# Two heads at a time: a change to the preparation of cluster-masked attention

## The chip, the cores and the metric

The kernel runs on one core of a Trainium2 chip. The metric is the device time in microseconds (us) of one execution, the median of the runs.

## The reference

Three blocks follow each other: attention in which a query sees only the keys of its own cluster, a feed-forward block with a squared ReLU, and a mixture of eight experts with a gate that is normalised over rows and columns eight times. Only the attention matters here:

```python
B, H, S, D = 2, 8, 768, 64          # 16 centroids for each head
q_n = q / (norm(q) + 1e-06); k_n = k / (norm(k) + 1e-06); c_n = centroids / (norm(centroids) + 1e-06)
q_assign = argmax(einsum('bhsd,hcd->bhsc', q_n, c_n), axis=-1)
k_assign = argmax(einsum('bhsd,hcd->bhsc', k_n, c_n), axis=-1)
mask = q_assign[:, :, :, None] == k_assign[:, :, None, :]
scores = where(mask, scale * matmul(q, k.transpose(0, 1, 3, 2)), -1e9)
attn = exp(scores - max(scores)); attn = attn / (sum(attn) + 1e-09)
out = matmul(attn, v)
```

## The kernel before

The attention stage works through 96 query tiles, six of 128 queries for each of 16 heads (`tile_steps`, L547). For each tile TensorE computes the scores of 128 queries against 768 keys (`score`, L448: four matmuls of 384 columns), VectorE takes the row maximum (L454), ScalarE the exponential (L461), TensorE transposes the result (L476, six transposes), ScalarE and VectorE take it out of PSUM as a high and a low part (L483, L489), and TensorE multiplies by the values (L501). Scores are issued three tiles ahead. High and low parts (`fp32r` tiles) stand in for one fp32 operand.

The mask is folded into the score matmul: the stacked operands `qb` and `kb` of a head hold 64 rows of data and 16 rows of marks, one for each centroid, which the preparation of the head computes. `prepare(n)` (L247) does so for a group of four heads, that is two pairs of heads; there are four groups. Its steps:

- `load`: four tiles of 128 rows (q and k of two heads each, transposed); `scale` multiplies the q tiles by 0.125; `high` (ScalarE, L268) and `low` (L273) split each.
- `sims` (L282): 24 matmuls multiply the split tiles by the split centroids. The centroid operand `z` is padded with zeros to 128 columns, so that all four tiles accumulate into the same output tile, one quarter of its partitions each.
- `turn` (L290) transposes that in 32 x 32 blocks on VectorE, `normal` (L297) multiplies by the inverse norms, `top` (L301) takes the maximum over 16 centroids, `match` (L305) compares, `back` (L309) transposes back, `earliest` (L316, L317) keeps the first of equal maxima by a matmul with a constant band, and `marks` copies 16 rows for each head into `qb` and `kb`.
- `norms` (L202) loads q and k in natural layout (`nat`), squares them, sums over 64 elements, and takes square root (L237), + 1e-6 and reciprocal.
- `stack` copies the high and low parts of a head into its stacked operands: six SBUF-to-SBUF DMAs.
- `vload` and `vsplit` bring in and split the values.

The first group is prepared before the first tile, the others beside the tiles. `plan` says for each step the tile behind which it is written; `SHIFT` and `MOVES` displace single steps by hand. For the first 72 tiles a planner orders each engine's instructions by its own estimate of when they can start, and the written order is the priority; from tile 72 on the written order holds. DMAs are issued on the SP queue, for two heads of the first group on GpSimd's queue.

Of the kernel before, what the change touches and what calls it, by code (L numbers as in the profile page):

```python
# [17 lines left out]
P = 128  # L18
# [23 lines left out]


MOVES = {
    (1, "low", 2): 2, (1, "match"): 1, (1, "sims", 1, 1): -1, (1, "turn", 1): -2, (2, "earliest", 0): -1,
    (2, "inverse"): 1, (2, "load", 1): -1, (2, "sims", 1, 1): -1, (3, "earliest", 0): -1,
    (3, "earliest", 1): -1, (3, "normal", 0): 1, (3, "sims", 0, 0): 1, (3, "sims", 1, 0): 1,
}
SHIFT = (
    {},  # L50
    dict(high=-1, low=-1, top=-1, match=-1, back=-1, vload=2, stack=-2),
    dict(
        high=-3, low=-3, sims=-3, turn=-3, top=-1, match=-1, back=-1, vload=1, vsplit=-1, stack=-1, square=-1, total=-1
    ),
    dict(high=-1, low=-1, sims=-2, turn=-2, normal=-1, vsplit=2, marks=1, square=-3, root=1),
)
# [6 lines left out]
class Kernel:  # L63
# [103 lines left out]
    def centroids(self, craw):  # L167
# [3 lines left out]
        z = self.tile("z", [P, 2, 4, 2, P], F32R, pool=self.prep)  # L171
        nc.vector.memset(f32(z), 0.0)
# [4 lines left out]
        nc.scalar.activation(ss, ss, AF.Sqrt)  # L177
        nc.vector.tensor_scalar_add(ss, ss, 1e-6)
# [10 lines left out]
        chi = self.tile("chi", [P, P], pool=self.prep)  # L189
        clo = self.tile("clo", [P, P], pool=self.prep)  # L190
        nc.vector.tensor_copy(chi.bitcast(F32R), ct[:, :P])
        nc.vector.tensor_tensor(clo, ct[:, :P], chi, op=ALU.subtract)
        for t in range(2):
            for qd in range(4):
                cols = slice(32 * (2 * t + qd // 2), 32 * (2 * t + qd // 2) + 32)
                nc.vector.tensor_copy(z[:, t, qd, 0, 32 * qd : 32 * qd + 32], chi[:, cols])
                nc.scalar.copy(z[:, t, qd, 1, 32 * qd : 32 * qd + 32], clo[:, cols])
        self.cst = z
# [3 lines left out]
    def norms(self, n, soon=False):  # L202

        nc = self.nc
        rn = self.rn[n] = self.tile("rn", [P, 24, 2], bufs=2, pool=self.prep)
        nats = {}

        def load(u):
            if n == 1:
                nats[u] = self.tile("atl" if u else "ath", [P, 12, 2, D], bufs=2)  # L210
            else:
                nats[u] = self.tile("nat", [P, 12, 2, D], bufs=2, pool=self.prep)
            b, t = divmod(n, 2)
            nc.sync.dma_start(nats[u], self.qkn[b, t, :, 12 * u : 12 * u + 12])

        def square(u):
            nat = nats[u]
# [5 lines left out]
        def total(u):  # L223
            nat = nats.pop(u)
            width = D
            while width > (1, 1, D, D // 2)[n] and n:
                width //= 2
                add = nat[:, :, :, :width]
                nc.gpsimd.tensor_tensor(add, add, nat[:, :, :, width : 2 * width], op=ALU.add)
            out = rn[:, 12 * u : 12 * u + 12]  # L230
            if width == 1:
                nc.gpsimd.tensor_copy(out.unsqueeze(3), nat[:, :, :, :1])
            else:
                nc.vector.reduce_sum(out, nat[:, :, :, :width], axis=AX.X)

        def root():
            nc.scalar.activation(rn, rn, AF.Sqrt)  # L237

        def inverse():
            add = nc.vector.tensor_scalar_add(rn, rn, 1e-6)  # L240
            if n == 1:
                self.tc.keep_in_program_order(add)
            nc.vector.reciprocal(rn, rn)

        return load, square, total, root, inverse

    def prepare(self, n, soon=False):  # L247
# [3 lines left out]
        b, t = divmod(n, 2)  # L251
        st = {}
        qa, qb, ka, kb, vv = self.heads_q, self.heads_qm, self.heads_k, self.heads_km, self.heads_v
        raw, hi, lo, vr = {}, {}, {}, {}
        alt = nc.vector if soon or n == 3 else nc.gpsimd
        busy = nc.vector if n < 2 else nc.gpsimd

        def load(qd):
            tag, bufs = ("eq", 1) if soon and qd == 3 else ("raw", 3)
            raw[qd] = self.tile(tag, [P, S], bufs=bufs, pool=self.prep)  # L260
            nc.sync.dma_start(raw[qd], self.qk[b, t, qd])

        def scale(qd):
            busy.tensor_scalar_mul(raw[qd], raw[qd], 0.125)

        def high(qd):
            hi[qd] = self.tile(f"hi{qd}", [P, S], F32R, pool=self.prep)
            nc.scalar.copy(hi[qd], raw[qd])  # L268

        def low(qd):  # L270
            lo[qd] = self.tile(f"lo{qd}", [P, S], F32R, pool=self.prep)
            eng = nc.gpsimd if qd % 2 else alt
            eng.tensor_tensor(lo[qd], raw.pop(qd), f32(hi[qd]), op=ALU.subtract)  # L273

        def sims(u, part):
            if part == 0:
                st[u] = self.ps("t", [P, 512])
            cols = slice(u * HALF, u * HALF + HALF)
            for qd in (2 * part, 2 * part + 1):
                zh, zl = self.cst[:, t, qd, 0], self.cst[:, t, qd, 1]  # L280
                for i, (z, x) in enumerate(((zh, hi[qd]), (zh, lo[qd]), (zl, hi[qd]))):
                    nc.tensor.matmul(  # L282
                        st[u][:, :HALF], z, x[:, cols], start=(qd == 0 and i == 0), stop=(qd == 3 and i == 2)
                    )

        def turn(u):
            if u == 0:
                st["sim"] = self.tile("sim", [P, 24, 2, C], pool=self.prep)
            flat = st["sim"].rearrange("p a j c -> p (a j c)")
            nc.vector.transpose(flat[:, u * HALF : u * HALF + HALF], st.pop(u)[:, :HALF])  # L290

        def wide(ap):
            return ap.unsqueeze(3).to_broadcast([P, 24, 2, C])

        def normal(u):
            cols = slice(12 * u, 12 * u + 12)
            alt.tensor_tensor(st["sim"][:, cols], st["sim"][:, cols], wide(self.rn[n])[:, cols], op=ALU.mult)  # L297

        def top():
            st["mx"] = self.tile("mx", [P, 24, 2], pool=self.prep)  # L300
            nc.vector.tensor_reduce(st["mx"], st["sim"], axis=AX.X, op=ALU.max)  # L301

        def match():
            st["eq"] = self.tile("eqb", [P, 24, 2, C], BF16, pool=self.prep)
            nc.vector.tensor_tensor(st["eq"], st["sim"], wide(st["mx"]), op=ALU.is_equal)  # L305

        def back():
            st["eqt"] = self.tile("eqt", [P, S], BF16, pool=self.prep)
            nc.vector.transpose(st["eqt"], st["eq"].rearrange("p a j c -> p (a j c)"))  # L309

        def earliest(u):
            if u == 0:
                st["rows"] = self.tile("eq", [P, S], pool=self.prep)
            ps = self.ps("t", [P, 512])
            cols = slice(u * HALF, u * HALF + HALF)
            nc.tensor.matmul(ps[:, :HALF], self.band, st["eqt"][:, cols], start=True, stop=True)  # L316
            nc.vector.tensor_scalar(st["rows"][:, cols], ps[:, :HALF], self.floor, self.floor, op0=ALU.add, op1=ALU.max)  # L317

        def stack(k):
            hd, (i, j) = 4 * n + k, divmod(k, 2)  # L320
            part = slice(64 * j, 64 * j + 64)
            q_hi, q_lo, k_hi, k_lo = hi[2 * i][part], lo[2 * i][part], hi[2 * i + 1][part], lo[2 * i + 1][part]
# [4 lines left out]
            for dst, src in (  # L327
# [3 lines left out]
                (nc.gpsimd if n == 0 and k > 1 else nc.sync).dma_start(f32(dst), f32(src))  # L331

        def marks(k):
            hd, (i, j) = 4 * n + k, divmod(k, 2)
            r0 = 64 * i + 16 * j
            rows = st["rows"]
            if hd == 0:
                nc.vector.tensor_copy(qb[hd][64:], rows[:16])
                nc.vector.tensor_copy(kb[hd][64:], rows[32:48])
                return  # L340
            nc.sync.dma_start(f32(qb[hd][64:]), rows[r0 : r0 + 16])
            nc.sync.dma_start(f32(kb[hd][64:]), rows[r0 + 32 : r0 + 48])

        def vload(i):
            vr[i] = self.tile("vraw", [P, QT, 2, D], bufs=2)
            nc.sync.dma_start(vr[i], self.v[b, 2 * t + i])

        def vsplit(k):
            i, j = divmod(k, 2)
            vt = vv[4 * n + k] = self.tile("vv", [P, QT, 2, D], F32R, bufs=4)  # L350
            busy.tensor_copy(vt[:, :, 0, :], vr[i][:, :, j, :])
# [782 lines left out]
```

## Time and profile before

| what | value |
|---|---|
| runs | 1570.94 us median of 3 (1569.94 to 1571.08) |
| profiled execution | 1570.48 us, of which the profile's span is 1568.7 us |
| TensorE busy | 1526.6 us (97% of the span) |
| VectorE, ScalarE, GpSimd busy | 898.7, 760.3 and 964.6 us (57%, 48% and 61%) |
| granted clock of TensorE | 0.995 of full speed over the span |

PE is TensorE, PEld its weight loads, DVE VectorE, ACT ScalarE, POOL GpSimd, SP the engine whose queue issues most DMAs. Busy time of matmuls is pipelined and their ends are modelled; the distance from start to start shows their pace.

### The profile page before, as it was taken

The numbers are of one execution on the slowest core, as the hardware profiler recorded it, in microseconds if no ns is written. First come the engines' busy times: TensorE is split into PE (matmuls) and PEld (weight loads), VectorE is DVE, ScalarE is ACT, GpSimd is POOL, SyncE is SP. The second block draws the span as 40 slices with busy tenths as digits, with TensorE's granted clock in tenths as the row PEclk, the third lists the DMA queues.
The fourth block names the chain that finished last, engine by engine and source line by source line (L and its number), as shares of the span: only waits on it lengthen the run. The fifth ranks groups of instructions, "written<-read, shape, count | busy, mean of one in ns | idle before, by whom it ended". The sixth has DMA issues, their size and how long they took to land.

```text
span 1568.7 us, 21863 instructions
## 1 busy us (share of the span) xinstructions
PE 1526.6 (97%) x8136; PEld 1399.6 (89%) x8136; DVE 898.7 (57%) x1573; ACT 760.3 (48%) x1416; POOL 964.6 (61%) x726
## 2 busy tenths in 40 slices
PE   4999998999999999999999999999999999999998
PEld 4888987999999988899999999999999999999997
DVE  7989889876653445644444535565445444444444
ACT  4889898866665643343333333333333333333331
POOL 5764446656664866656566666677565757575652
PEclk8999999999999999999999999999999999999999
DMA  9864440122220011112121211213121212121211
GB/s 276 196 188 102 97 125 29 54 81 81 81 108 0 1 55 68 67 54 81 56 80 58 77 66 69 78 57 121 55 81 55 81 55 81 54 81 55 81 55 41
DMA packets 26793, 124.69 MB, mean 79 GB/s; under 512 B 4448, under 2 KB 4576, under 8 KB 16448
## 3 DMA queue, kind: packets, MB, share of 16 engines
q1 hardware_dynamic: 26112, 120.95, 23.9%
q0 software_dynamic: 576, 2.36, 0.7%
q8 instruction: 64, 1.05, 0.3%
q14 instruction: 41, 0.34, 0.1%
HBM read 99.80 MB, written 3.15 MB: 66 GB/s over the span
## 4 chain that ended last, share of the span: by engine, by line
PE 87%; ACT 4%; DVE 3%; POOL 2%; issue 2%; DMA 1%; SPq 0%; ACTq 0%; POOLq 0%; DVEq 0%
PE t L135 34%; PE s L985 22%; PE y L985 11%; PE s L705 7%; PE s L448 3%; PE pv L501 3%; PE u L135 2%; PE t L476 2%; ACT e L461 1%; PE u L476 1%; DVE atl L489 1%; DVE m L454 1%; ACT ath L483 1%; POOL fa L623 0%; DMA ka<-hi 0%
## 5 line engine op out<-in xcount | busy, mean ns | idle before, releaser
L964 ACT ACTIVATE hh<-c 128x384 fp32r<-128x384 f32 x256 | 134.6, 526 | 606.1 <-PE y L985 266.4
L892 POOL TENSOR_TENSOR wl<-raw,wh 128x1024 fp32r<-128x1024 f32 x64 | 155.3, 2427 | 348.2 <-ACT wh L891 348.2
L965 DVE SCALAR_TENSOR_TENSOR hl<-c,hh 128x384 fp32r<-128x384 f32 x256 | 174.8, 684 | 172.5 <-ACT hh L964 172.5
L985 PE MATMUL s<-wh,hh 128*128 128x512 f32 x512 | 201.2, 393 | 0.0
L985 PE MATMUL s<-wl,hh 128*128 128x512 f32 x512 | 200.6, 392 | 0.0
L985 PE MATMUL s<-wh,hl 128*128 128x512 f32 x512 | 200.3, 391 | 0.0
L135 PE MATMUL t<-th,ah 128*128 128x384 f32 x512 | 171.8, 336 | 0.8 <-DVE c L1059 0.8
L135 PE MATMUL t<-tl,ah 128*128 128x384 f32 x512 | 172.0, 336 | 0.0
L135 PE MATMUL t<-th,al 128*128 128x384 f32 x512 | 171.8, 336 | 0.0
L884 POOL TENSOR_TENSOR al<-sm,ah 128x1024 fp32r<-128x1024 f32 x64 | 156.6, 2447 | 3.5 <-ACT ah L881 3.4
L882 POOL TENSOR_TENSOR al<-raw,ah 128x768 fp32r<-128x768 f32 x64 | 137.8, 2153 | 0.0
L135 PE MATMUL t<-xh,ah 128*128 128x384 f32 x384 | 129.4, 337 | 0.1
L135 PE MATMUL t<-xh,al 128*128 128x384 f32 x384 | 129.2, 336 | 0.0
L135 PE MATMUL t<-xl,ah 128*128 128x384 f32 x384 | 129.0, 336 | 0.0
L1035 DVE TENSOR_TENSOR c<-t,c 128x384 f32<-128x384 f32 x64 | 35.7, 558 | 144.9 <-PE t L135 144.9
L985 PEld LDWEIGHTS s<-wh,hl 128*128 128x128 f32 x512 | 96.1, 188 | 21.1
L985 PEld LDWEIGHTS s<-wh,hh 128*128 128x128 f32 x512 | 96.2, 188 | 11.7
L985 PEld LDWEIGHTS s<-wl,hh 128*128 128x128 f32 x512 | 96.2, 188 | 11.3
L691 POOL TENSOR_TENSOR hl<-r,hh 128x384 fp32r<-128x384 f32 x64 | 74.3, 1162 | 49.3 <-ACT r L690 46.1
L985 PE MATMUL y<-wh,hl 128*128 128x512 f32 x256 | 99.7, 390 | 0.0
L985 PE MATMUL y<-wh,hh 128*128 128x512 f32 x256 | 99.7, 389 | 0.0
L985 PE MATMUL y<-wl,hh 128*128 128x512 f32 x256 | 99.6, 389 | 0.0
(231 smaller groups left out, 4019.2 us busy)
## 6 DMA issues: line engine op xcount, KB each, us to landing
raw<-in_w SPq DMA_DIRECT2D x64, 1024.0 KB, 4.8
wraw<-in_w SPq DMA_DIRECT2D x16, 1024.0 KB, 4.9
raw<-in_qk SPq DMA_DIRECT2D x15, 384.0 KB, 5.1
ka<-hi SPq DMA_DIRECT2D x28, 192.0 KB, 3.7
nat<-in_qkn SPq DMA_DIRECT2D x6, 768.0 KB, 7.7
vraw<-in_v SPq DMA_DIRECT2D x8, 384.0 KB, 4.8
out<-x SPq DMA_DIRECT2D x12, 256.0 KB, 2.0
qa<-hi SPq DMA_DIRECT2D x14, 192.0 KB, 2.6
```

The costliest lines, as they stand in the source:

```text
L135: self.nc.tensor.matmul(out, a, b, start=(i == 0), stop=(i == n - 1))
L448: nc.tensor.matmul(s[:, u, :HALF], a[:, qs], k[:, u * HALF : u * HALF + HALF], start=(a is qa), stop=(a is qb))
L476: nc.tensor.transpose(t[:, k, :], e[:, kt * P : kt * P + P], self.ident)
L501: nc.tensor.matmul(o, vt[:, kt].rearrange("p a d -> p (a d)"), aT[half][w][:, kt, :], start=(kt == 0 and w == 0), stop=(kt == QT - 1 and w ...
L691: nc.gpsimd.tensor_tensor(hl, r, f32(hh), op=ALU.subtract)
L705: nc.tensor.matmul(o, a, b, start=(start and i == 0), stop=(stop and i == 2))
L882: nc.gpsimd.tensor_tensor(al[:, : 3 * Q], raw[:, : 3 * Q], f32(ah[:, : 3 * Q]), op=ALU.subtract)
L884: nc.gpsimd.tensor_tensor(al[:, 3 * Q :], self.sums.rearrange("p a b -> p (a b)"), f32(ah[:, 3 * Q :]), op=ALU.subtract)
L892: nc.gpsimd.tensor_tensor(wl, raw[:, 1024:], f32(wh), op=ALU.subtract)
L964: nc.scalar.activation(hh, c, AF.Relu)
L965: nc.vector.scalar_tensor_tensor(hl, c, 0.0, f32(hh), op0=ALU.max, op1=ALU.subtract)
L985: nc.tensor.matmul(ys[t][m], a, b, start=(start and i == 0), stop=(stop and i == 2))
```

## The change

`prepare(p)` and `norms(p)` now serve one pair of heads, so there are eight of them instead of four, each with tiles of half the width, and all are made by one list of steps at offsets from tile 10(p - 1); `MOVES` and `SHIFT` are gone. Only pair 0 is prepared before the first tile; of pair 1 the loads and the square stand there too.

Similarities are computed in plain fp32 from the unsplit tiles: four matmuls for a pair, each with 32 centroid columns, each into another quarter of the output's partitions (two halves of the sequence, for q and k), instead of 24 padded matmuls for two pairs. The split and padded centroids are gone; one unsplit copy stays.

The square root of the squared norm is now exp(0.5 ln(x + 1e-30)). The table set that holds both functions is loaded once, behind the centroids' square root.

Engines: `scale`, `normal` and the first part of `vsplit` run on VectorE for pair 0 and on GpSimd for the others; `low` runs on GpSimd but for the first of pair 0. Sums have one halving add on GpSimd for each pair but the first. `marks` are four copies for each head instead of two (on VectorE and ScalarE for head 0, DMAs otherwise). All stack DMAs are on the SP queue.

```diff
-MOVES = {
...
-SHIFT = (
...
+        self.tiny = per.tile([P, 1], F32, name="tiny")
+        nc.vector.memset(self.tiny, 1e-30)
...
-        z = self.tile("z", [P, 2, 4, 2, P], F32R, pool=self.prep)
-        nc.vector.memset(f32(z), 0.0)
...
         nc.scalar.activation(ss, ss, AF.Sqrt)
+        self.tc.keep_in_program_order(nc.scalar.preload_act_table_set("natural_log_exp_and_others"))
...
+        self.cst = self.tile("cent", [P, P], pool=self.prep)
+        nc.vector.tensor_copy(self.cst, ct[:, :P])
...
+    def norms(self, p, soon=False):
...
+        def nload():
+            st["nat"] = self.tile("nat", [P, 12, 2, D], bufs=2, pool=self.prep)
+            nc.sync.dma_start(st["nat"], self.qkn[p // HP, p % HP])
...
+        def total():
+            nat = st.pop("nat")
+            rn = self.rn[p] = self.tile("rn", [P, 12, 2], bufs=2, pool=self.prep)
             width = D
+            if p:
+                width = D // 2
+                nc.gpsimd.tensor_tensor(
+                    nat[:, :, :, :width], nat[:, :, :, :width], nat[:, :, :, width:], op=ALU.add
+                )
+            nc.vector.reduce_sum(rn, nat[:, :, :, :width], axis=AX.X)
 
         def root():
-            nc.scalar.activation(rn, rn, AF.Sqrt)
+            rn = self.rn[p]
+            log = nc.scalar.activation(rn, rn, AF.Ln, bias=self.tiny)
+            if p == 0:
+                self.tc.keep_in_program_order(log)
+            nc.scalar.activation(rn, rn, AF.Exp, scale=0.5)
...
+    def prepare(self, p, soon=False):
...
+        busy = nc.gpsimd if p else nc.vector
...
+        def low(i):
+            lo[i] = self.tile(f"lo{i}", [P, S], F32R, bufs=2, pool=self.prep)
+            eng = nc.gpsimd if p or i else nc.vector
+            eng.tensor_tensor(lo[i], raw[i], f32(hi[i]), op=ALU.subtract)
 
-        def sims(u, part):
...
-                for i, (z, x) in enumerate(((zh, hi[qd]), (zh, lo[qd]), (zl, hi[qd]))):
...
+        def sims():
+            ps = st["ps"] = self.ps("t", [P, 512])
+            z = self.cst[:, 32 * hp : 32 * hp + 32]
+            for u in range(2):
+                for i in range(2):
+                    r = 64 * u + 32 * i
                     nc.tensor.matmul(
+                        ps[r : r + 32, :HALF], z, raw[i][:, u * HALF : u * HALF + HALF], start=True, stop=True
                     )
...
+        def normal():
+            busy.tensor_tensor(st["sim"], st["sim"], wide(self.rn.pop(p)), op=ALU.mult)
...
+            for u in range(2):
+                for i, to in enumerate((qb[hd], kb[hd])):
+                    r = 64 * u + 32 * i + 16 * j
+                    dst, src = to[64:, u * HALF : u * HALF + HALF], rows[r : r + 16]
+                    if hd == 0 and i:
+                        nc.vector.tensor_copy(dst, src)
+                    elif hd == 0:
+                        nc.scalar.copy(dst, src)
+                    else:
+                        nc.sync.dma_start(f32(dst), src)
...
+        pairs = [self.prepare(p, soon=p < 2) for p in range(B * HP)]
+        one, two = pairs[:2]
+        one["load"](0)
+        one["load"](1)
+        one["nload"]()
+        two["load"](0)
+        two["load"](1)
         self.more_constants()
+        one["scale"]()
+        for i in range(2):
+            one["high"](i)
+            one["low"](i)
+        one["stack"](0)
+        two["nload"]()
+        one["vload"]()
+        one["stack"](1)
         self.centroids(craw)
...
+        for name in ("square", "sims", "turn", "total", "root", "inverse", "normal", "top", "match", "back", "earliest"):
+            one[name]()
+        for j in range(2):
+            one["marks"](j)
+        two["square"]()
...
+        at(-1, 0, "vsplit", 0)
+        at(2, 0, "vsplit", 1)
+        for p in range(1, B * HP):
+            s = 10 * (p - 1)
+            if p > 1:
+                for d, *st in ((-6, "load", 0), (-6, "load", 1), (-5, "nload"), (-3, "square")):
+                    at(s + d, p, *st)
+            for d, *st in (
+                (-1, "scale"), (-1, "total"), (0, "high", 0), (1, "low", 0), (1, "high", 1), (2, "low", 1), (1, "root"),
+                (2, "inverse"), (2, "sims"), (3, "turn"), (4, "normal"), (5, "top"), (5, "match"), (6, "back"),
+                (7, "earliest"), (3, "stack", 0), (8, "marks", 0), (9, "stack", 1), (9, "marks", 1),
+            ):
+                at(s + d, p, *st)
+            at(12 * p - 12, p, "vload")
+            for j in range(2):
+                at(12 * p + 6 * j - 8, p, "vsplit", j)
```

## Rows read from the trace of the kernel before

**Rows 1.** Windows: start:end, length, busy us of PE, PEld, DVE, ACT, POOL; PEclk, DMA.

```profile
0.00:29.60 29.60, 10.45 (x34) 9.07 (x35) 23.43 (x44) 12.95 (x21) 16.20 (x25) 0.88 0.95 284
29.60:240.00 210.40, 200.96 (x1262) 182.04 (x1262) 188.32 (x347) 184.08 (x408) 113.65 (x103) 0.98 0.60 143
240.00:285.00 45.00, 40.47 (x257) 35.89 (x256) 40.24 (x73) 37.03 (x82) 26.75 (x23) 1.00 0.13 48
```

**Rows 2.** Timeline of VectorE, 44 to 49 us: start, length, engine, line.

```profile
46.43 0.95 DVE L454 TENSOR_REDUCE m<-s 128x1 f32<-128x768 f32 x1
...
48.23 0.95 DVE L454 TENSOR_REDUCE m<-s 128x1 f32<-128x768 f32 x1
```

**Rows 3.** Timeline of TensorE, 65.4 to 66.5 us.

```profile
65.52 0.49 PE L516 MATMUL t<-cst,rsum 128*64 128x128 f32 x3
65.84 0.49 PE L476 MATMUL t<-cst,e 128*128 128x128 f32 x3
```

**Rows 4.** The chain that ended last, 170 to 190 us: start, length.

```profile
181.86 2.11 PE u L282 x12
```

**Rows 5.** Timeline of the first 30 us.

```profile
6.66 0.83 ACT L268 CAST hi<-raw 128x768 fp32r<-128x768 f32 x1 [0.40 <-DMA raw<-in_qk]
...
7.58 1.80 POOL L273 TENSOR_TENSOR lo<-raw,hi 128x768 fp32r<-128x768 f32 x1 [6.65 <-ACT hi L268]
7.66 2.13 DVE L264 TENSOR_SCALAR raw<-raw 128x768 f32<-128x768 f32 x1 [0.40 <-DMA raw<-in_qk]
...
12.25 2.85 ACT L219 ACTIVATE nat<-nat 128x1536 f32<-128x1536 f32 x2
...
17.96 1.71 DVE L234 TENSOR_REDUCE rn<-nat 128x24 f32<-128x1536 f32 x1
...
19.70 0.24 ACT L237 ACTIVATE rn<-rn 128x48 f32<-128x48 f32 x1 [3.22 <-DVE rn L234]
...
20.69 1.13 DVE L297 TENSOR_TENSOR sim<-sim,rn 128x384 f32<-128x384 f32 x2
...
28.57 1.65 PE L448 MATMUL s<-kb,qb 80*128 80x384 f32 x4 [0.97 <-DVE kb L339]
```

**Rows 6.** DMA issues, 0 to 30 us: KB each, median us to landing.

```profile
kb<-lo SPq DMA_DIRECT2D x2, 192.0 KB, 8.3
```

**Rows 7.** Groups by line, 0 to 285 us: busy us, mean ns, idle before.

```profile
L234 DVE TENSOR_REDUCE rn<-nat 128x24 f32<-128x1536 f32 x4 | 6.9, 1722 | 0.0
L273 DVE TENSOR_TENSOR lo<-raw,hi 128x768 fp32r<-128x768 f32 x4 | 4.2, 1059 | 0.0
L264 DVE TENSOR_SCALAR raw<-raw 128x768 f32<-128x768 f32 x4 | 4.0, 992 | 1.5 <-DMA raw<-in_qk 1.5
L351 DVE CAST vv<-vraw 128x384 fp32r<-128x384 f32 x8 | 3.6, 448 | 0.0
L234 DVE TENSOR_REDUCE rn<-nat 128x24 f32<-128x768 f32 x2 | 1.9, 946 | 0.0
...
L461 ACT ACT_TABLE_LOAD x3 | 3.8, 1283 | 0.1
L237 ACT ACT_TABLE_LOAD x2 | 2.6, 1283 | 0.0
...
L273 POOL TENSOR_TENSOR lo<-raw,hi 128x768 fp32r<-128x768 f32 x11 | 20.5, 1870 | 19.6 <-ACT hi L268 12.0 <-DMA kb<-lo 4.6 <-PE s L448 2.7
L221 POOL TENSOR_TENSOR nat<-nat 128x1536 f32<-128x1536 f32 x4 | 11.1, 2772 | 1.8 <-DMA nat<-in_qkn 1.8
L264 POOL TENSOR_SCALAR raw<-raw 128x768 f32<-128x768 f32 x4 | 8.5, 2132 | 2.6 <-DMA raw<-in_qk 2.6
L229 POOL TENSOR_TENSOR nat<-nat 128x768 f32<-128x768 f32 x2 | 3.9, 1938 | 0.2
```

**Rows 8.** Timeline of TensorE, 631 to 632 us: the gate's fp32 matmul.

```profile
631.29 0.46 PE L773 MATMUL t<-pm,ones 128*128 128x96 f32 x2
631.54 0.48 PE L985 MATMUL s<-wh,hh 128*128 128x512 f32 x1
```

More of the change, by code (lines that the diff above doesn't have):

```diff
@@ L41 @@
 BIG = 2.0 ** 100
-MOVES = {
[L45 to L48, printed above, removed]
-SHIFT = (
[L50 to L56, printed above, removed]
 def f32(ap):
@@ L188, in centroids, with square @@
         nc.tensor.transpose(ct[:, :P], cn.rearrange("p j d -> p (j d)"), self.ident)
[L189 to L202, printed above, removed]
-        nc = self.nc
[L205 to L217, printed above, removed]
+        self.cst = self.tile("cent", [P, P], pool=self.prep)
+        nc.vector.tensor_copy(self.cst, ct[:, :P])
+    def norms(self, p, soon=False):
+        nc = self.nc
+        st = {}
+        def nload():
+            st["nat"] = self.tile("nat", [P, 12, 2, D], bufs=2, pool=self.prep)
+            nc.sync.dma_start(st["nat"], self.qkn[p // HP, p % HP])
+        def square():
+            nat = st["nat"]
             if soon:
@@ L266, in high @@
[L266 to L273, printed above, removed]
-        def sims(u, part):
[L276 to L280, printed above, removed]
-                for i, (z, x) in enumerate(((zh, hi[qd]), (zh, lo[qd]), (zl, hi[qd]))):
+        raw, hi, lo = {}, {}, {}
@@ L319, in stack @@
-        def stack(k):
-            hd, (i, j) = 4 * n + k, divmod(k, 2)
+            nc.tensor.matmul(ps[:, :HALF], self.band, st["eqt"], start=True, stop=True)
+            nc.vector.tensor_scalar(st["rows"], ps[:, :HALF], self.floor, self.floor, op0=ALU.add, op1=ALU.max)
+        def stack(j):
+            hd = 2 * p + j
             part = slice(64 * j, 64 * j + 64)
-            q_hi, q_lo, k_hi, k_lo = hi[2 * i][part], lo[2 * i][part], hi[2 * i + 1][part], lo[2 * i + 1][part]
+            q_hi, q_lo, k_hi, k_lo = hi[0][part], lo[0][part], hi[1][part], lo[1][part]
@@ L330, in stack, with marks @@
             ):
[L331 to L335, printed above, removed]
+                nc.sync.dma_start(f32(dst), f32(src))
+        def marks(j):
+            hd = 2 * p + j
             rows = st["rows"]
[L337 to L351, printed above, removed]
-            nc.gpsimd.tensor_tensor(vt[:, :, 1, :], vr[i][:, :, j, :], f32(vt[:, :, 0, :]), op=ALU.subtract)
-        return [
-            (-4, load, 0), (-4, load, 1), (-4, load, 2), (2, load, 3), (-2, scale, 0), (-1, scale, 2),
-            (1, high, 0), (2, high, 1), (2, low, 0), (3, low, 1), (4, high, 2), (4, low, 2), (5, high, 3), (6, low, 3),
-            (6, sims, 0, 0), (7, sims, 0, 1), (8, turn, 0), (8, sims, 1, 0), (9, sims, 1, 1), (10, normal, 0),
-            (10, turn, 1), (11, normal, 1), (13, top), (14, match), (16, back), (17, earliest, 0), (18, earliest, 1),
-            (6, vload, 0), (13, vsplit, 0), (16, vsplit, 1), (20, vload, 1), (22, vsplit, 2), (28, vsplit, 3),
-            (14, stack, 0), (16, stack, 1), (18, marks, 0), (18, marks, 1),
-            (19, stack, 2), (19, marks, 2), (22, stack, 3), (22, marks, 3),
-        ]
@@ L364, in attention, with vsplit @@
+        def vsplit(j):
+            vt = vv[2 * p + j] = self.tile("vv", [P, QT, 2, D], F32R, bufs=4)
+            busy.tensor_copy(vt[:, :, 0, :], st["vr"][:, :, j, :])
+            nc.gpsimd.tensor_tensor(vt[:, :, 1, :], st["vr"][:, :, j, :], f32(vt[:, :, 0, :]), op=ALU.subtract)
+        steps = (
+            load, scale, high, low, sims, turn, normal, top, match, back, earliest, stack, marks, vload, vsplit
+        )
+        return {x.__name__: x for x in steps + self.norms(p, soon)}
     def attention(self):
@@ L369, in attention @@
         plan = {}
-        first = self.prepare(0, soon=True)
-        norm0, norm1 = self.norms(0, soon=True), self.norms(1, soon=True)
         craw = self.tile("craw", [P, D], pool=self.prep)
         nc.sync.dma_start(craw, self.cent)
-        def run(*names):
-            for st in first:
-                if st[1].__name__ in names:
-                    st[1](*st[2:])
-        run("load")
-        for u in range(2):
-            norm0[0](u)
-        for u in range(2):
-            norm1[0](u)
@@ L385, in attention @@
-        self.more_constants()
-        run("scale", "high", "low")
-        def some(name, *ks):
-            for st in first:
-                if st[1].__name__ == name and st[2] in ks:
-                    st[1](*st[2:])
-        some("stack", 0, 1)
-        some("vload", 0)
-        some("stack", 2, 3)
-        second = self.prepare(1)
-        for st in second[:3]:
-            st[1](*st[2:])
-        self.centroids(craw)
-        for u in range(2):
-            norm0[1](u)
-        for u in range(2):
-            norm0[2](u)
@@ L404, in attention @@
-        norm0[3]()
-        norm0[4]()
-        for u in range(2):
-            norm1[1](u)
-            norm1[2](u)
-        norm1[3]()
-        run("sims", "turn", "normal", "top", "match", "back", "earliest")
-        run("marks")
-        for g, *what in (
-            (-1, "vsplit", 0), (2, "vsplit", 1), (2, "vload", 1), (6, "vsplit", 2), (10, "vsplit", 3)
-        ):
-            plan.setdefault(g + MOVES.get((0, *what), 0), []).append([*[x for x in first if [x[1].__name__, *x[2:]] == what][0][1:]])
```

87 lines of the change are left out of this document (28 added, 59 removed).

## Prediction

> **What bounds the kernel now.** I read the windows by stage first, because the diff touches only the attention stage and what stands in front of it [rows 1]. Before 29.6 us there is a start in which TensorE is busy 10.45 us of 29.60; from 29.6 to about 285 us the 96 query tiles run; behind that come the experts, which the diff doesn't touch and which merely begin earlier or later. So the gain or loss is a sum of two terms: how much earlier the first tile begins, and how long 96 tiles take.
>
> In the tile loop no engine stands clear of the others: from 29.6 to 240 us TensorE is busy 201 of 210.4 us, VectorE 188, ScalarE 184, GpSimd only 114 [rows 1]. Busy time of pipelined matmuls overstates TensorE, so I take paces from start to start. A tile alone costs VectorE 1.80 us (two row maxima start at 46.43 and 48.23 with the tile's two subtractions between them) [rows 2]. On TensorE three transposes take 0.32 us from start to start [rows 3], and twelve 384-column matmuls 2.11 us, 0.176 us each [rows 4]; a tile has eight of these, six transposes and one small transpose for the row sums, so 8 x 0.176 + 7 x 0.107 = 2.16 us. The loop runs at (285 - 29.6) / 96 = 2.66 us a tile. The 0.5 us between that and TensorE's own pace is preparation of later heads on all engines and the hitches it makes: few buffers stand between score, exponential, transposes and subtraction. I therefore count work taken off TensorE or VectorE in the loop at about half its size, and work of GpSimd at nothing as long as nobody waits for it.
>
> **The start.** The first score's second half begins at 28.57 us, after a chain over two pairs of heads: [rows 5] two squares on ScalarE (2.85 us from 12.25), two sums on VectorE (the second from 17.96, 1.71 us), root at 19.70, normalisation from 20.69, and then maximum, match, transposes, prefix matmul and marks to 28.57. Squares start only at 12.25 because ScalarE is held by four splits, the last of them fed late.
>
> With one pair, the norm input is the third large load instead of the fifth. The second key-or-query load is there at 6.66, the third at 7.66 [rows 5], so 384 KB take about 1.0 us and the 768 KB of norms should be in at about 6.7 + 2.0 = 8.7 us. ScalarE has only two splits by then (0.83 us each). From there: one square 1.43 (half of 2.85), one sum 1.71, root and inverse 1.2 (0.99 from 19.70 to 20.69, and one more ScalarE instruction of 0.24), then the 7.88 us from 20.69 to 28.57 at half the columns, 3.94. The end is 8.7 + 1.43 + 1.71 + 1.2 + 3.94 = 17.0 us. Another path could end later: head 0's last stacked copy needs the low part of k, which GpSimd finishes at 7.58 + 1.80 = 9.4 us [rows 5], and such a copy took 8.3 us to land in this crowded stretch [rows 6], so 17.7 us. I take 17.6: **11.0 us earlier**. Bounds: 12 us if the copy is quicker with less traffic ahead; 7.7 us if the last 7.88 us don't shrink at all (fixed costs of short operations, four mark copies in place of two): 28.57 - (13.04 + 7.88).
>
> That moves work into the loop, for pair 1 was prepared by 28.57 before and now is prepared beside the first tiles.
>
> **VectorE in the loop** [rows 5, 7]. Gone: two lows of the last group (1.06 each, 2.1), two scales (at most 2.0; I take 1.3, as one of the four shown took 2.13 [rows 5]), six v casts (0.45 each, 2.7), one group's two normalisations (1.13 [rows 5]). The sums go from two of 1.72 and two of 0.95 (5.3) to seven of 0.95 (6.6): +1.3. Pair 1's own turn, maximum, match, turn back and floor come in: about 3. Inverses on shorter tiles, seven instead of two in the loop: about +1. Sum -1.9 us.
>
> **ScalarE in the loop.** Four table loads of 1.283 us go (two roots, each with a load and a load back [rows 7]; the third load under the exponential's line lies at the start), 5.1 us. In come seven logarithms and seven exponentials instead of two roots, 12 x 0.24 = 2.9, and two more splits, 1.7. Sum -0.5 us; but a load blocks the engine for 1.28 us in one piece, which the short ones don't.
>
> The Trainium skill (ScalarE: Activation LUTs, "What ACT_TABLE_LOAD costs") puts a switch at about 2.66 us with its drain. The rows show 1.283 us of load; by the page the four switches would be 10.6 us instead of 5.1, and the forecast some 3 us lower.
>
> **TensorE in the loop.** 72 matmuls of 0.176 us go (three groups of 24): -12.7 us [rows 4]. In come 28 matmuls, four for each of seven pairs, in plain fp32 with 32 weight columns, each into another quarter of the output partitions. The trace has no such thing. The nearest is the gate's fp32 matmul of 96 columns: two records, and the next matmul starts 0.25 us after the first [rows 8]. Scaled by columns, 384 cost at most 1.0 us. If the four run one after the other: 4.0 us a pair, 28 us, net +15.3. If they run side by side: 1.0 a pair, 7 us, net -5.7. No row shows two matmuls side by side. I take the lower end, since the four have separate weights and outputs and wait for nothing of each other, and keep the upper one as a rival.
>
> The Trainium skill (TensorEngine Tiling (Array Packing), "Key Properties") says that tiles of different columns load and multiply in parallel, and that a change of tiling mode drains the engine. By the first rule the net is -5.7 us, by the second something comes back at both ends of each of the seven groups; no run shown here prices it.
>
> **GpSimd and SP.** GpSimd takes over two squares (2.77), three scales (2.13), four lows in the loop (1.87), five adds in the loop (1.94), some 29 us [rows 7], and three normalisations and six v casts, each shorter than a low; with 35 us it goes from 114 to about 149 of 210 us [rows 1], 71%. What hides it is that free time, and that heads are prepared tiles ahead: pair p begins at tile 10(p - 1), its first head is scored at tile 12p - 3, and its first marks are planned for tile 10p - 2. That leaves 2p - 1 tiles: one for pair 1, three for pair 2. Marks now take four copies a head instead of two, 28 more on SP behind the stack copies; between 29.6 and 240 us the DMA engines are busy 0.60 of the time [rows 1], so I cost them at nothing. Without that cover, pair 1 stalls scoring at tile 9 for up to a tile, 2.66 us.
>
> Half of TensorE's -5.7 and VectorE's -1.9 is -3.8; ScalarE's -0.5 and its unbroken flow I count at -0.5; one stall of half a tile for pair 1 gives back 1.3. **Loop: -3.0 us**. Bounds: -8 (all savings in full, no stall) and +10 (half of +15.3, a whole stall, nothing saved elsewhere).
>
> **Sum.** 1570.48 (the profiled execution) - 11.0 - 3.0 = 1556.5 us. The median of the runs is 0.46 us above that execution, so 1557 us, 0.9% less. Faster or slower by 0.2%, about what a measurement of this kernel can tell, is 3.1 us: below 1567.8 or above 1574.1.
>
> **Rivals.**
>
> *The four fp32 matmuls run one after the other.* For it: the 0.25 us of the gate's matmul; against it: separate quarters. In the loop +21 us of TensorE against my sum, at half +10.5; at the start 4 us of them come before the first turn, at a lower clock longer (0.88 granted on average before 29.6 [rows 1]), which takes some 3 us of the gain there. 1557 + 13.5 = 1570.5 us.
>
> *GpSimd hands over late (slower).* Three steps of each pair now have VectorE or ScalarE waiting in order for GpSimd: scale before the high part, add before the sum, normalisation before the maximum. If at two of the three the waiting engine stands behind one low (1.87 us [rows 7]), seven pairs lose 26 us, and row maxima and exponentials queue behind it: 1557 + 26 = 1583. It decides for slower from (1574.1 - 1557) / 7 = 2.4 us a pair. For it: GpSimd is the one engine that gains work, and its steps are now closer together. Against it: in the loop it is idle nearly half the time now [rows 1].
>
> A second form of it is in the Trainium skill (SBUF — State Buffer, "SBUF: two separate sides"): GpSimd and some VectorE operations share a port pair as an exclusive lock. The start agrees (a VectorE scale of 2.13 us beside a GpSimd low from 7.58 to 9.38 [rows 5]); but the tile's own maximum and subtractions, which read PSUM, kept to 1.80 us [rows 2], and the change takes scales and casts off VectorE.
>
> *Logarithm and exponential do not share a table.* Then each pair loads twice, 14 loads of 1.283 us [rows 7] where I count none, 18 us on ScalarE; counted at half to full, 1566 to 1575, say 1570. Against it: squares and casts in this trace cause no load beside either table.
>
> *Everything counts in full.* Start -12, loop -8: 1551.
>
> **How the numbers follow.** Forecast 0.60 (its own range 1551 to 1563), everything in full 0.08, matmuls in series 0.15, late hand-over 0.13, separate tables 0.04. Series splits 0.04 faster, 0.11 same; tables same; late hand-over slower. Faster 0.72, same 0.15, slower 0.13. The range 1548 to 1573 leaves out late hand-over and part of separate tables, under 0.2 in all.
>
> **What would show it.** Right: the first row maximum near 18.5 us instead of 29.6; four similarity matmuls of a pair starting within 0.2 us; two table loads in all; loop from the first maximum to the last subtraction some 3 us shorter than before; expert stage unchanged in length. Wrong: matmuls of one group starting 0.5 us or more apart; idle time of VectorE or ScalarE put down to GpSimd's scale, add or normalisation; scoring of tile 12 waiting for a mark copy by more than a tile; any load between logarithm and exponential.

## The result and the profile after

The changed kernel takes **1589.98 us** (median of 4 runs, 1589.03 to 1592.65), the kernel before 1570.59 in the same comparison: ratio 1.0126 [1.0109, 1.0144], slower by 19.4 us where 1557 was predicted. The profiled execution took 1589.97 us with a span of 1588.2.

The windows of the changed kernel, cut at its first row maximum, at 240 us and at the end of the tile loop, answer to [rows 1]:

```profile
core 0: us, PE busy (x) PEld busy (x) DVE busy (x) ACT busy (x) POOL busy (x), PEclk, DMA share, GB/s
0.00:21.20 21.20, 4.82 (x17) 2.68 (x18) 11.60 (x28) 8.84 (x12) 7.94 (x9) 1.00 0.92 263
21.20:240.00 218.80, 189.37 (x1145) 162.40 (x1145) 172.85 (x335) 167.54 (x379) 123.37 (x99) 0.95 0.55 141
240.00:302.60 62.60, 57.18 (x359) 50.55 (x359) 54.35 (x99) 53.80 (x121) 38.84 (x38) 1.00 0.19 69
```

In the loop the three engines that the tiles keep busiest are busy a smaller share of the time than before: VectorE 79% (90% in [rows 1]), TensorE 87% (96%), ScalarE 77% (87%). GpSimd, which gained work, went from 54% to 56%. Nothing became the bound by its amount of work; the engines wait for each other more. TensorE's granted clock averages 0.95 of full speed here.

Where the time went, between marks that both traces have (first and last row maximum, first second-layer matmul of the experts, last matmul):

| stage | before | after | difference | forecast |
|---|---|---|---|---|
| to the first row maximum | 29.6 | 21.2 | -8.4 | -11.0 |
| first to last row maximum | 246.8 | 272.8 | +25.9 | -3.0 |
| experts, to that matmul | 296.9 | 296.6 | -0.3 | 0 |
| blocks | 991.2 | 993.6 | +2.4 | 0 |

They sum to +19.6; the spans differ by 19.5. So the start did most of what was expected, and the loop misses by 29 us.

**The loop.** What engines waited for, 30 to 300 us, from the list of waits of the changed kernel (us in total, times, longest):

```profile
...
DVE rn L206 <- POOL nat L203: 22.6, 6, 4.8
PEld t L426 <- DVE atl L439: 20.4, 16, 4.6
...
DVE atl L439 <- ACT ath L433: 18.0, 34, 2.4
```

The first line shown is the sum of a pair's squares on VectorE, waiting for GpSimd's addition of halves. Before, such sums waited for nothing [rows 7]. One of the six, on GpSimd's timeline of the changed kernel:

```profile
69.51 2.32 POOL L237 TENSOR_SCALAR raw<-raw 128x768 f32<-128x768 f32 x1
76.18 1.84 POOL L246 TENSOR_TENSOR lo<-raw,hi 128x768 fp32r<-128x768 f32 x1 [4.36 <-ACT hi L241]
77.99 2.74 POOL L195 TENSOR_TENSOR nat<-nat 128x1536 f32<-128x1536 f32 x1
80.70 1.02 POOL L485 TENSOR_TENSOR x<-xb,rs 64x384 f32<-64x384 f32 x1
81.69 1.78 POOL L203 TENSOR_TENSOR nat<-nat 128x768 f32<-128x768 f32 x1
```

and on VectorE's:

```profile
78.51 0.54 DVE L439 TENSOR_TENSOR atl<-u,ath 128x384 fp32r<-128x384 f32 x1
83.50 0.95 DVE L206 TENSOR_REDUCE rn<-nat 128x24 f32<-128x768 f32 x1 [4.45 <-POOL nat L203]
84.37 0.55 DVE L439 TENSOR_TENSOR atl<-t,ath 128x384 fp32r<-128x384 f32 x1
84.83 0.95 DVE L404 TENSOR_REDUCE m<-s 128x1 f32<-128x768 f32 x1
```

and on ScalarE's:

```profile
84.49 0.31 ACT L210 ACTIVATE rn<-rn,tiny 128x24 f32<-128x24 f32 x1 [3.65 <-DVE rn L206]
84.83 0.22 ACT L213 ACTIVATE rn<-rn 128x24 f32<-128x24 f32 x1
```

GpSimd first stands 4.36 us waiting for ScalarE's high part, then makes the low part, the square, a tile's output and only then the addition. VectorE has reached the sum at 79.05 and stands until 83.50, with the next tiles' subtractions and row maxima behind it; ScalarE stands 3.65 us at the logarithm, with exponentials behind that. GpSimd's free time (44% of the loop) is of no use here: it is idle *ahead* of the late step. It could have squared in that time, for the data of the square were there. From the instructions of that tile, 60 to 90 us:

```profile
L188 SPq DMA_DIRECT2D nat<-in_qkn x1: 327/327/327, 64.6 to 64.6; - x1
...
DMA to landing us min/median/max: 7.0/7.0/7.0
```

The load landed at 71.6 us, as GpSimd began to stand, and the square began at 77.99. The plan lists the square two tiles ahead of the scale and four ahead of the first low part; in the order that GpSimd executed, it stands behind both, in all six pairs.

TensorE's clock fell soon after the waits. Two of its stretches at the lower of its two levels (1.2 GHz, 0.50 in the column PEclk):

```profile
84.80:91.60 6.80, 6.15 (x24) 5.34 (x25) 6.12 (x14) 4.38 (x11) 1.46 (x2) 0.50 0.87 188
...
176.90:183.70 6.80, 5.51 (x22) 5.22 (x23) 5.04 (x11) 3.94 (x11) 4.82 (x6) 0.50 0.55 123
```

There are five such stretches in the loop, 23.9 us in all. Four of them begin within 2 us of the end of one of the six waits; in the 4 us ahead of each fall TensorE was busy between 0.12 and 1.83 us.

**The start.** From VectorE's timeline of the changed kernel, against [rows 5]:

```profile
9.99 1.75 DVE L206 TENSOR_REDUCE rn<-nat 128x24 f32<-128x1536 f32 x1
13.70 0.68 DVE L217 TENSOR_SCALAR rn<-rn 128x24 f32<-128x24 f32 x1 [1.96 <-ACT rn L213]
...
14.75 1.77 DVE L266 TENSOR_TENSOR sim<-sim,rn 128x384 f32<-128x384 f32 x1
```

and from ScalarE's:

```profile
8.47 1.48 ACT L193 ACTIVATE nat<-nat 128x1536 f32<-128x1536 f32 x1
11.63 1.56 ACT L241 CAST hi<-raw 128x768 fp32r<-128x768 f32 x2 [1.67 <-POOL raw L237]
13.10 0.31 ACT L210 ACTIVATE rn<-rn,tiny 128x24 f32<-128x24 f32 x1
```

Load, square and sum came as worked out (square from 8.47, sum from 9.99 to 11.74). The logarithm then stood 1.36 us behind two splits that ScalarE takes in order, themselves fed late by GpSimd's scale; and the steps from normalisation to score took 5.40 us (14.75 to 20.15) where 3.94 was expected. The two splits belong to pair 1, which the first tile does not need. The chain that ended last runs through them (start, length):

```profile
3.04 6.34 DMA raw<-in_qk
...
9.46 2.14 POOL raw L237
...
11.63 1.56 ACT hi L241 x2
13.19 0.23 ACT rn L210
```

So a load of pair 1 decides when the first tile begins. Three of the kernels below (sum later, sum at s, norms early) have the same instructions in the same order up to the first row maximum. In them and in the changed kernel it comes at 20.9 to 23.4 us, so one profile tells the start to some 2.5 us.

The four fp32 matmuls of a pair, from TensorE's timeline of the changed kernel (each leaves two records):

```profile
31.58 0.85 PE L254 MATMUL t<-raw,cent 128*32 128x384 f32 x8
32.36 0.45 PE L451 MATMUL pv<-ath,vv 128*128 128x384 f32 x1
```

All four take 0.78 us up to the next matmul's start: side by side. Table loads are two in the whole program, as predicted.

### The profile page after: what moved, and what is told of

Its sections match the earlier page's. It is cut to its first block, busy times and chain, and to the rows that moved or that the text cites. A ratio compares the mean times of both kernels' runs of the same rounds, so it can differ in the third digit from the quotient of the medians.

```text
span 1588.2 us, 21807 instructions
## 1 busy us (share of the span) xinstructions
PE 1528.1 (96%) x8104; PEld 1389.0 (87%) x8104; DVE 932.1 (59%) x1571; ACT 756.3 (48%) x1416; POOL 975.2 (61%) x722
## 4 chain that ended last, share of the span: by engine, by line
PE 83%; DVE 5%; POOL 5%; ACT 4%; issue 2%; DMA 0%; SPq 0%; POOLq 0%; ACTq 0%; DVEq 0%
PE t L120 34%; PE s L935 22%; PE y L935 11%; PE s L655 7%; PE u L120 2%; PE s L398 2%; PE pv L451 2%; DVE atl L439 1%; DVE m L404 1%; PE t L426 1%; ACT e L411 1%; POOL nat L195 1%; POOL lo L246 1%; ACT ath L433 1%; POOL nat L203 1%
## 5 line engine op out<-in xcount | busy, mean ns | idle before, releaser
L915 DVE SCALAR_TENSOR_TENSOR hl<-c,hh 128x384 fp32r<-128x384 f32 x256 | 224.3, 877 | 164.6 <-ACT hh L914 164.6
L120 PE MATMUL t<-th,al 128*128 128x384 f32 x512 | 172.5, 337 | 0.0
L834 POOL TENSOR_TENSOR al<-sm,ah 128x1024 fp32r<-128x1024 f32 x64 | 166.3, 2599 | 3.9 <-ACT ah L831 3.8
L832 POOL TENSOR_TENSOR al<-raw,ah 128x768 fp32r<-128x768 f32 x64 | 126.7, 1980 | 0.0
L935 PEld LDWEIGHTS s<-wh,hl 128*128 128x128 f32 x512 | 96.1, 188 | 21.2
```

Source lines behind the costliest of these rows:

```text
L120: self.nc.tensor.matmul(out, a, b, start=(i == 0), stop=(i == n - 1))
L832: nc.gpsimd.tensor_tensor(al[:, : 3 * Q], raw[:, : 3 * Q], f32(ah[:, : 3 * Q]), op=ALU.subtract)
L834: nc.gpsimd.tensor_tensor(al[:, 3 * Q :], self.sums.rearrange("p a b -> p (a b)"), f32(ah[:, 3 * Q :]), op=ALU.subtract)
L915: nc.vector.scalar_tensor_tensor(hl, c, 0.0, f32(hh), op0=ALU.max, op1=ALU.subtract)
L935: nc.tensor.matmul(ys[t][m], a, b, start=(start and i == 0), stop=(stop and i == 2))
```

## The experiments

Two theories for the loop. **A**: the sum stands in VectorE's order ahead of the moment at which GpSimd can have added. **B**: GpSimd has too much work, wherever the sum stands. Unless said otherwise each kernel is the changed one with the edit shown; "loop" is first to last row maximum in its profiled execution.

**Sum two tiles later, GpSimd as it is.** The sum becomes a step of its own, held at tile s+2 of pairs 2 to 7; root to marks follow it.

```
- (-1, "total"), ... (1, "root"), (2, "inverse"), ... (4, "normal"), (5, "top"), ...
+ (-1, "total"), (2, "add_up"), (3, "root"), (4, "inverse"), (5, "normal"), (6, "top"), ...
```

> The changed kernel with the VectorE sum of pairs 2 to 7 pinned behind tile 10(p-1)+2 instead of planned at tile 10(p-1)-1, and root, inverse, normalisation, maximum, match, turn back, floor and marks one or two tiles later; GpSimd's work and its order stay. Theory A (VectorE stands in its order behind GpSimd's late halving add: 22.6 us of idle time in six pairs) expects that idle time under 6 us and 1568 to 1576 us. Theory B (GpSimd has too much work, wherever one waits for it) expects the idle time to come back at the normalisation or the splits and 1584 us or more.

1565.33 us, ratio to before 0.9957 [0.9942, 0.9972], better still than A had it; loop 248.0. The group of the sum in the changed kernel, from its groups by line (busy us, mean ns, idle before):

```profile
L206 DVE TENSOR_REDUCE rn<-nat 128x24 f32<-128x768 f32 x7 | 6.7, 952 | 22.6 <-POOL nat L203 22.6
```

and here:

```profile
L212 DVE TENSOR_REDUCE rn<-nat 128x24 f32<-128x768 f32 x7 | 6.6, 937 | 0.0
```

22.6 us of standing went, and 24.7 us of loop with it: loop and wait shrink by about the same. The half-speed stretches shrank too, from 23.9 to 3.5 us, so these 24.7 us hold what the lower clock cost as well.

**Sum at s, two tiles earlier than in that kernel.** One place changed: `(2, "add_up")` to `(0, "add_up")` for the same pairs.

> The kernel of e1 with VectorE's sum pinned two tiles earlier (at the pair's tile s instead of s+2), nothing else changed. Theory A (VectorE reaches the sum before GpSimd has added, and stands): in e1 the add ends, unhindered, about 1.3 tiles behind row maximum s+12-12, at tile 13.3 on average counted as 12 for the second pair, and the sum in the changed kernel stood at 11.7 to 11.8. At about 12.5 the wait should be 0.8 tile of 2.6 us for six pairs, some 12 us: median 1572 to 1580, waits of the sum for the add 8 to 16 us. Rival C (holding the sum in place at all changed the order of the rest, and its place does not matter): 1564 to 1567, no such waits.

1572.76 us, ratio 1.0008 [0.9996, 1.0019]; loop 253.7.

```profile
L212 DVE TENSOR_REDUCE rn<-nat 128x24 f32<-128x768 f32 x7 | 6.6, 949 | 7.2 <-POOL nat L203 7.2
```

The time is within what A gave, the wait (7.2) a little under its 8 to 16. Wait and loop go together over three kernels: 0.0 and 248.0, 7.2 and 253.7, 22.6 and 272.8. C falls. This kernel spent 3.4 us at half speed, as little as the one with the sum at s+2, so its 5.7 us of longer loop are the price of 7.2 us of wait without the clock.

**The other end moved: GpSimd squares and adds three tiles earlier.** The work is that of the changed kernel. The norm load is listed four tiles earlier, and VectorE's sum, part of the same step as the addition, three tiles earlier too.

```
- (-5, "nload"), (-3, "square"), ... (-1, "total")
+ (-9, "nload"), (-6, "square"), (-4, "total")
```

> The changed kernel with norm load, square, add and sum of pairs 2 to 7 planned three to four tiles earlier, so that GpSimd does square and add ahead of the pair's scale and lows; the same work. Theory A expects the idle time of VectorE before the sum under 6 us and 1566 to 1576 us. Theory B expects 1584 us or more, since GpSimd does as much as before.

1568.88 us, ratio 0.9971 [0.9957, 0.9985]; loop 249.7, the sum idle 0.9 us in one place. Next the same with the sum held at s-1, so that only GpSimd's side moves, and without the constant tile (below):

> The kernel of e7 with the distance between add and sum made the other way: squares and adds three tiles earlier on GpSimd (as in e5), the sum held at its listed place s-1, root to marks at the steps of the changed kernel. Theory A (only the distance of sum from add counts, not which of them moved): no waits of the sum for the add, loop 247 to 250 us, median 1563 to 1567. Rival: it is the later root, normalisation and maximum of e7 that helped (less for VectorE to hand on at once): 1570 or more.

1566.30 us, ratio 0.9969 [0.9956, 0.9982]; loop 250.1, no wait of the sum for the addition. GpSimd does the same work as in the slow kernel, and the sum stands where it stood there, so B falls; it is the distance between the two steps.

**Less for GpSimd, more for VectorE.** The better kernel without the addition: VectorE sums all 64 columns.

> The kernel of e7 without GpSimd's add of halves: VectorE sums all 64 columns, 1.72 us for 0.95 (7 x 0.77 = 5.4 us more on VectorE), GpSimd loses 7 x 1.94 = 13.6 us. Theory A (GpSimd's amount of work costs nothing once nobody waits for it; VectorE's counts about half): 1567 (1565 to 1569). Rival B (GpSimd's amount of work still delays): faster than e7, 1558 to 1563.

1569.28 us, ratio 0.9983 [0.9974, 0.9992], against 0.9959 for the kernel it changes: some 4 us slower (the intervals leave 1 to 6). B, which had this kernel faster, falls again: 13.6 us less for GpSimd did not pay for 5.4 us more for VectorE. If GpSimd's were worth nothing, VectorE's cost about 0.7 of their size, where half was counted; the run does not price the two apart.

**What the parts are worth once nobody waits.** The first experiment's kernel with twelve zero-padded fp32r matmuls a pair in place of four fp32 ones (the low part is left out of the similarities):

```
- nc.tensor.matmul(ps[r : r + 32, :HALF], z, raw[i][:, ...], start=True, stop=True)
+ for k in range(3):
+     nc.tensor.matmul(ps[:, :HALF], z_padded, hi[i][:, ...], start=..., stop=...)
```

> The kernel of e1 with the similarities of a pair made by twelve matmuls in fp32r with weights padded by zeros to 128 columns (as before the change, 384 columns each) in place of four side by side; the moving operand is the high part in all twelve, so the low part is left out of the similarities. TensorE has 7 x (12 x 0.176 - 0.85) = 8.8 us more in the loop. By the prediction's counting (half of TensorE's time counts) the median goes to 1569.7 (1568.5 to 1572). Rival: in this loop TensorE's time counts for little against the order in which engines wait for each other: 1565 to 1567.

1568.29 us, ratio 0.9977 [0.9966, 0.9987], loop 250.0: between the two, some 3 us (by the ratios; the intervals overlap) for 8.8 us of TensorE: about a third, which these intervals do not tell from the half. The same kernel with a square root in place of logarithm and exponential:

> The kernel of e1 with one square root per pair in place of logarithm and exponential: two table loads of 1.28 us more for each of seven pairs, 14 in all, some 18 us on ScalarE, less seven short instructions of 0.24 us. Counted at half, as the prediction counts ScalarE: 1573 (1570 to 1577). Rival: as with the kernel before, where removing four loads gained nothing, the loads fall beside other waits: under 0.3 us for each load, 1565 to 1569.

1571.84 us, ratio 1.0006 [0.9996, 1.0015], loop 253.7: some 7 to 8 us for 16.3 us of ScalarE. Its 14 loads, from its groups by line:

```profile
L215 ACT ACT_TABLE_LOAD x7 | 9.0, 1283 | 0.1
L415 ACT ACT_TABLE_LOAD x7 | 9.0, 1283 | 0.1
```

Half a microsecond of program for 1.28 us of load: here the prediction's half was right, and the rival falls. ScalarE is idle for some 0.02 us before each of these loads and as little behind it, so a switch takes 1.3 us of ScalarE here, and not the 2.66 us that the prediction quotes beside its sum.

**The parts alone, on the kernel before.** Logarithm and exponential alone:

> The kernel before with the square root as logarithm and exponential alone (table set loaded once behind the centroids' root). The forecast's term (four table loads of 1.283 us in the loop less four short instructions, counted at about half) expects 1 to 3 us less than before, 1567.5 to 1569.5 us, and two table loads in all. If the loads block the loop in full, 4 to 5 us less. If the norms by logarithm cost anything themselves, the same or slower.

1572.59 us, ratio 1.0012 [1.0002, 1.0022]: a miss. Its loop is 247.2 against 246.8; four loads removed gained nothing there, and its blocks are 2.3 us longer, which is the next experiment's matter. Column tiles alone, with four buffers for the raw loads where there were three:

> The kernel before with similarities alone as fp32 matmuls of 32 weight columns into four quarters (eight matmuls for a group instead of 24, one more buffer for raw tiles). Side by side as in the changed kernel's trace (0.85 us for four) TensorE has 3 x (4.2 - 1.7) = 7.5 us less in the loop; the forecast counts half: with some 3 us at the start 1563 to 1567 us. If TensorE is not what the loop waits for: only the start's 2 to 4 us.

1577.28 us, ratio 1.0035 [1.0022, 1.0048], loop 255.9: a miss too. 6.2 us of the 9 are lost by tile 12. ScalarE's timeline in this kernel:

```profile
42.33 0.22 ACT L450 ACTIVATION_READ_ACCUMULATOR e<-s,m 128x1 f32 x1
47.27 0.83 ACT L258 CAST hi<-raw 128x768 fp32r<-128x768 f32 x1 [4.73 <-issue]
48.01 0.47 ACT L472 CAST ath<-t 128x384 fp32r<-128x384 f32 x1
```

A split stands 4.73 us, with the tiles' casts behind it; that split waited 0.48 in the kernel before. The profile names nothing that ends this wait ("issue"); the chain that ended last runs to it through two stack copies (8.23 and 4.12 us), which read tiles that splits write. Whether the fourth buffer, with its earlier loads, made the copies late was not tried, so this run does not price the matmuls.

**The blocks.** Every kernel with the constant tile `tiny` (four bytes a partition) has blocks of 993.5 or 993.6 us, every one without it 991.2. The kernel with the square root keeps the tile and has 993.5 too, so it is not the logarithm. The first experiment's kernel without it:

```
- log = nc.scalar.activation(rn, rn, AF.Ln, bias=self.tiny)
+ log = nc.scalar.activation(rn, rn, AF.Ln)
```

> The kernel of e1 without the four-byte-wide constant tile that the logarithm's bias reads (bias 0 instead of 1e-30), so that everything behind it in memory lies where it lay before the change. Theory P (place in memory): in the runs with this tile the subtraction that makes hl takes 2.2 us in 35 or so of 256 places where it took 0.88 before, its mean is 877 to 902 ns instead of 684, and the stage of the blocks is 2.3 us longer; without the tile the mean falls back to about 684 ns, the stage to 991.2 us, and the median to 1563.0 (1562 to 1564). Rival: the length comes with logarithm and exponential themselves (the kernel with these alone has it too): mean stays near 890 ns and the median at 1565.3.

1564.45 us, ratio 0.9959 [0.9946, 0.9972]; blocks 991.2 us, mean of that subtraction 683 ns. The stage follows P exactly. The median lies near P's, but a start 1.4 us later in the profiled execution and the spread of the runs (1562.55 to 1566.09) hide 2 us: by ratios the two kernels can't be told apart.

**Scale listed one tile earlier** in that kernel:

> The kernel of e7 with GpSimd's scale of each pair listed one tile earlier. In e7 ScalarE still waits 5.0 us in three places for the scale. If that is what keeps its loop (248.2 us) from being the 3 us shorter than before that the prediction had, the median goes from 1564.5 to 1560 (1558 to 1563); if these waits lie beside others, 1563 to 1566.

1564.81 us, ratio 0.9953 [0.9941, 0.9966], loop 248.4: no difference. The waits of ScalarE for the scale stayed at 4.9 us, so the step's new place in the list did not bring the hand-over forward, and the question stays open.

The best kernels, sum two tiles later with or without `tiny`, beat both: 0.4% faster than before, some 1.6% faster than the changed one.

## Why the prediction was wrong

**The step that failed** is "What hides it is that free time, and that heads are prepared tiles ahead", with GpSimd's work counted at nothing. It holds for the amount of work (giving GpSimd 13.6 us less gained nothing on balance) and fails for the place. The plan lists a pair's addition and sum as one step at s-1, two tiles behind the square; GpSimd executes scale, low part, square, a tile's output and addition in this order (2.32 + 1.84 + 2.74 + 1.02 + 1.78 = 9.7 us in the rows above) with a wait for ScalarE in between. Counted in row maxima, the additions ended, and VectorE's sums began, at 11.8, 21.8, 31.8, 41.7, 51.8 and 61.9; in the first experiment, where VectorE goes on meanwhile, the same additions end at 13.0, 23.9, 33.9, 42.0, 53.4 and 63.3. That is 1.5 tiles further in the mean, which at 2.6 us a tile is the 3.8 us of a wait. "Tiles ahead" was true of the marks, not of this hand-over.

**The rival** of late hand-over was right in kind: 26 us at 3.7 us a pair were named, 22.6 us in six pairs measured, 3.8 each, and its 1583 us is 7 from the result. That the size fits so well is luck. It put one low part (1.87 us) in front of each of two places; the runs show one place, the addition before the sum, with several steps in front of it. The scale before the high part cost ScalarE 4.3 us in two places. "In the loop it is idle nearly half the time now" was no argument against it, and 0.13 was too low a chance.

**The start** was right in its chain up to the sum and 2.6 us too good: -8.4 for -11.0, in a profile that tells it to some 2.5 us. The load was there 0.2 us earlier than its term; square and sum were within 0.1 us of theirs. What was missed is that the logarithm stands behind two splits of pair 1, which wait for GpSimd's scale (+1.4, late hand-over again). Root and inverse took 1.65 us for 1.2, and the last steps 5.40 for 3.94 (+1.5). Of this +1.2 is the normalisation, 1.77 us beside two GpSimd subtractions where two such took 1.13 before [rows 5]. The steps behind it did about halve. The other path, by head 0's last copy, is not in the chain.

**TensorE** in the loop: the sum took the lower end, side by side at 1.0 us a pair; measured 0.78. "Matmuls in series" falls. The Trainium skill (TensorEngine Tiling (Array Packing), "Key Properties") has tiles load and multiply in parallel, and the trace agrees, with its 0.78 us. The half at which TensorE was counted measured about a third.

**ScalarE and VectorE**: two loads in all, so separate tables fall. A load is worth 0.5 us in the changed order and nothing in the order before; VectorE's time counts at about 0.7. The sums of work themselves were right. Windows of the whole loop, first of the kernel before, then of the first experiment:

```profile
29.60:277.40 247.80, 234.14 (x1470) 211.11 (x1469) 223.70 (x407) 215.76 (x477) 138.36 (x123) 0.98 0.52 128
22.80:271.80 249.00, 230.50 (x1455) 199.46 (x1454) 222.14 (x422) 215.30 (x486) 159.96 (x134) 0.99 0.53 138
```

VectorE has 1.6 us less (1.9 forecast), ScalarE 0.5 less as forecast; GpSimd gained 21.6 us, not 35.

**What stays open.** With the wait gone the loop is 248.0 us, 1.2 longer than before, where -3.0 was forecast and the prices measured above give -3.5 (a third of 5.7, 0.7 of 1.9, half of 0.5). What takes these 4 to 5 us is not settled, but the row maxima tell where they go: up to tile 60 the first experiment's loop is 4.6 us ahead of the loop before, and from there to tile 72 it takes 32.9 us against 26.8. In that stretch the kernel before finishes its last group (3.3 us of VectorE's work) while the changed one prepares pair 7. ScalarE's waits for the scale (4.9 us) are another candidate, which the one try did not move. The changed loop's granted clock (0.95, against 0.99 from 23 to 240 us with the sum later) was lower where TensorE stood idle more; its part in the 25.9 us was not separated from the wait's. An estimate: at the 5.7 us for 7.2 us of wait measured with the sum at s, 22.6 us would cost 18, and some 7 of the 24.7 us would be the clock's. The forecast had no term for a clock that falls in the loop.

## What to carry to other kernels

Free time of the engine that takes over a step says nothing about when it hands over: lay out its order, as executed and not as listed, from the last thing that releases it to the step that is waited for, in microseconds, and set that against the place at which the waiting engine, which runs in order, has the next instruction. Where the two stand in one list entry, split them, and move the consumer later (or the producer earlier) by the tiles that come out; here two tiles turned 1.3% slower into 0.4% faster with no work changed. A wait in front of this saturated loop cost about its own length, with the clock that it brought down. The 13.6 us of work on the engine with slack bought nothing on balance, and work on the fuller engines was paid at a third to 0.7 of its size, each figure from one pair of kernels and rough.

## What the runs showed of the hardware

The 2.3 us in the blocks, which nothing in the diff touches, hang on a few nanoseconds. VectorE's subtraction `hl` and GpSimd's subtraction `al` start at nearly the same moment there, 49 times. In the first experiment's kernel without the constant tile (all engines' timeline):

```profile
704.25 0.55 DVE L920 SCALAR_TENSOR_TENSOR hl<-c,hh 128x384 fp32r<-128x384 f32 x1
...
704.29 2.23 POOL L837 TENSOR_TENSOR al<-raw,ah 128x768 fp32r<-128x768 f32 x1
```

and in the first experiment's kernel, with the tile:

```profile
702.57 1.85 POOL L840 TENSOR_TENSOR al<-raw,ah 128x768 fp32r<-128x768 f32 x1
702.57 2.26 DVE L923 SCALAR_TENSOR_TENSOR hl<-c,hh 128x384 fp32r<-128x384 f32 x1
```

Where VectorE is some 15 to 60 ns ahead it takes 0.55 us and GpSimd 2.2; where GpSimd is ahead or level, VectorE is mostly held until GpSimd has ended, 2.24 to 2.27 us, and GpSimd takes 1.85. Before the change VectorE is ahead in all 49 places; with the tile, in the first experiment's kernel, 35 of 49 go the other way, and the mean of all 256 rises from 684 to about 890 ns. VectorE has slack there (172.5 us of idle time stand in front of these subtractions before the change), so 50 us of longer subtractions cost 2.3. The short case takes 0.55 us, not the 0.88 of the expectation above.

The Trainium skill (SBUF — State Buffer, "SBUF: two separate sides") describes such an exclusive lock: of a VectorE and a GpSimd operation that need the shared ports, the first has them for its whole length. The trace agrees, 0.55 against 2.26 us. That taking out one small tile turns the order was shown; why it moves the two starts by those nanoseconds was not.
